# The order of the opening's loads, early pieces of the first gate products, and the bank of the third gate product in a fused attention and SwiGLU kernel

## The chip, the core and the metric

The kernel runs on one core of a Trainium2 chip. The metric is device time in microseconds. TensorE (PE) multiplies matrices into PSUM, ScalarE (ACT) evaluates functions, VectorE (DVE) does elementwise work, GpSimd (POOL) here only issues loads, and SyncE (SP) issues stores and transposing DMAs.

## What is computed

Sliding-window attention with a linear bias over 8 batches of 8 heads, 576 positions and 64 dimensions. Its output, 4608 tokens of 512 numbers, goes through a SwiGLU block.

```python
B, H, S, D = q.shape                                  # 8, 8, 576, 64
scores = np.matmul(q, k.transpose(0, 1, 3, 2)) / np.sqrt(D)
rel = pos[:, None] - pos[None, :]
mask = (rel >= 0) & (rel < 128)
scores = np.where(mask, scores - slopes[:, None, None] * np.abs(rel), -1e9)
attn = softmax(scores)
x = np.matmul(attn, v).transpose(0, 2, 1, 3).reshape(B * S, H * D)   # 4608 x 512
g, val = x @ w_gate, x @ w_val                        # 512 x 1536 each
out = (g * sigmoid(g) * val) @ w_out                  # 1536 x 512
```

## The kernel before

Attention works in tiles of 128 queries with all 8 heads. There are 36 tiles, nine for each pair of batches; the ninth holds the last 64 positions of both. A tile needs q, k and v of its rank, a block of 128 positions, and k and v of the rank before it. Its steps are these. q and k are transposed into `qT` and `kT` (L194 to L219: PE transposes into a bank `pt`, then a copy by VectorE, or by ScalarE for k from rank 4). The `scores` are multiplied into banks `ps` or `psc`, and ScalarE takes the exponential into `ex` (L288) or `exc` (L322). From tile 4 on VectorE multiplies by a mask (L294, L326). `weighted` (L330) multiplies with v into `av`, and VectorE divides into `x` (L353, L354). `x_transposed` (L364) puts x, transposed by PE through a bank `px`, into `xT`.

The feed-forward part works on blocks of 512 tokens, so block 0 is made of tiles 0 to 3 and block 1 of tiles 4 to 7. For each of 12 slices m of 128 columns, `wide` (L395) makes the gate product `pg` and the value product `pv`, four matmuls each. ScalarE takes a tanh of `pg` (`tt`, L421), VectorE makes `uu` (L422) and the product `hT` with `pv` (L433). `project` (L452) multiplies block 0's hT with the output weights into a bank `po`; later blocks use a form with seven products for eight.

A product can be made in pieces: `wide(n, m, which, c1)` makes the columns up to c1 that are still missing, and `early` remembers where it stopped. `begin(n, tiles)` (L822) does so for the first n of (m = 0 gate, m = 0 value, m = 1 gate, m = 1 value, ...). In `first_tiles` (L828) the opening's order is written by hand for PE, VectorE and ScalarE: after the scores of all four tiles, tile 3's `weighted`, then x of tile 2, `begin(4, 2)`, x of tile 3 and `begin(4, 3)`. The first eight steps of `ffn` (m = 0 to 3 of block 0) are in that hand order too. After them a scheduler interleaves the attention of later tiles with `ffn`, and `scored`, `target` and `ready` in the driver set how many attention steps go with each step of `ffn`. PE, VectorE and ScalarE each run their own queue in order, so whatever stands behind a waiting instruction waits as well.

All PSUM is in two pools. `ps_f` has the tag "gv" with three banks in rotation (pg, pv, and in the opening pt, av) and the tag "po" with one bank (in the opening pt of some q and px of tiles 0 to 3, later the projections). `ps_a` has the tag "a" with four banks (ps, psc, and from tile 4 on pt, av and px; also pg and pv of m = 0 and 1 of block 0, which `OTHER` names at L393). A bank is free again when its reader is done: for pg that is uu, for pv hT.

The loads of q, k, v and the weights are issued by POOL in the order of the program (L893 to L927), with eight in flight at a time: the trace gives them eight semaphores in turn, and a ninth is issued after the first has landed. They convert to 16 bits on the way. A load of q, k or v writes 128 KB, a piece of 256 gate or value columns 256 KB, four row blocks of the output weights 512 KB.

Of the kernel before, what the change touches and what calls it, by code (L numbers as in the profile page):

```python
# [10 lines left out]
FP32 = mybir.dt.float32  # L11
# [5 lines left out]
P = 128  # L17
# [10 lines left out]
FIRST = 4  # L28
# [10 lines left out]
def slot(h):  # L39

    return 4 * (h // 4) + 2 * (h % 2) + (h % 4) // 2
# [9 lines left out]
def kernel(  # L51
# [45 lines left out]
    def first_masks():  # L97
        nc.vector.tensor_copy(idf, idm)
        for h in by_slot:
            nc.scalar.mul(bias[:, slot(h), :], dist, -(2.0 ** (-8.0 * (h + 1) / H)) / scale)  # L100

    def later_masks():
        for h in by_slot:
            nc.scalar.activation(reg[:, slot(h), :], dist, AF.Exp, scale=-(2.0 ** (-8.0 * (h + 1) / H)))
# [36 lines left out]
    ps_f = ctx.enter_context(tc.tile_pool(name="ps_f", bufs=3, space=PSUM))  # L141
    ps_a = ctx.enter_context(tc.tile_pool(name="ps_a", bufs=4, space=PSUM))
# [26 lines left out]
    def source(src, rank):  # L169

        s, c = divmod(rank, 9)
        if c == 8:
            return [((64 * n, 64 * n + 64),
                     src[2 * s + n, :, 512:576, :].rearrange("h p d -> p h d")) for n in range(2)]
        b, t = 2 * s + c // 4, c % 4
        return [((0, P), src[b, :, t * P:(t + 1) * P, :].rearrange("h p d -> p h d"))]

    def load_v(rank):
        va[rank] = va_all[rank % NV]
        for (p0, p1), src in source(v, rank):  # L180
            nc.gpsimd.dma_start(va[rank][p0:p1, :, 0:D], src)  # L181

    def load_qk(rank, which="kq"):
        for name in which:
            t_ = nat.tile([P, H, D], FP16, name=name + "n", tag=name + "n")
            for (p0, p1), src in source(k if name == "k" else q, rank):
                nc.gpsimd.dma_start(t_[p0:p1], src)  # L187
            (natk if name == "k" else natq)[rank] = t_
# [141 lines left out]
    def weighted(i):  # L330

        s, p = units[i]
        x = xpool.tile([P, H, D], FP16, name="x", tag="x")
        xs[i] = x
        for half in range(2):
            pool, tag = (ps_f, "gv") if i < FIRST else (ps_a, "a")
            av = pool.tile([P, 4, D + 1], FP32, name="av", tag=tag)
            todo = []
            for j in range(4):
                h = 4 * half + j  # L340
                if p == 8:
                    for n, kt in enumerate((3, 7, 8)):
                        todo.append((j, ex[(s, "c", n)][:, slot(h), :], va[9 * s + kt][:, h, :]))
                else:
                    if p not in (0, 4):
                        todo.append((j, ex[(s, p - 1)][:, slot(h), 128:256],
                                     va[9 * s + p - 1][:, h, :]))
                    todo.append((j, ex[(s, p)][:, slot(h), 0:128], va[9 * s + p][:, h, :]))
            for n, (j, w, val) in enumerate(todo):
                nc.tensor.matmul(av[:, j, :], w, val, start=(n == 0), stop=(n == len(todo) - 1))  # L350
            rec = xpool.tile([P, 4, 1], FP32, name="rec", tag="rec", bufs=4)
            with tc.high_priority() if i in (6, 7) else ExitStack():
                nc.vector.reciprocal(rec, av[:, :, D:D + 1])  # L353
                nc.vector.tensor_mul(x[:, 4 * half:4 * half + 4, :], av[:, :, 0:D],  # L354
                                     rec.broadcast_to([P, 4, D]))
# [3 lines left out]
    def place(i):  # L359

        s, p = units[i]
        return (8, s) if p == 8 else (2 * s + p // 4, p % 4)

    def x_transposed(i):  # L364
        n, j = place(i)
        if n not in xT:
            xT[n] = bpool.tile([P, NKB, 512], FP16, name="xT", tag="xTc" if n == 8 else "xT",
                               bufs=1 if n == 8 else 3)
        x = xs.pop(i).rearrange("p h d -> p (h d)")
        dst = xT[n][:, :, j * P:(j + 1) * P]  # L370
        if i >= X_DMA_FROM:
            nc.sync.dma_start_transpose(dst, x)
            return
        pool, tag, n = (ps_f, "po", 1) if i < FIRST else (ps_a, "a", 4)
        pt = pool.tile([P, NKB, P], FP16, name="px", tag=tag, bufs=n)
        for kb in range(NKB):
            nc.tensor.transpose(pt[:, kb, :], x[:, kb * P:(kb + 1) * P], idm if i < FIRST else idm2)
        if i < FIRST:
            nc.vector.tensor_copy(dst, pt)
        else:  # L380
            nc.scalar.copy(dst, pt)
# [11 lines left out]
    OTHER = {(0, 0, "g"), (0, 0, "v"), (0, 1, "g"), (0, 1, "v")}  # L393

    def wide(n, m, which, c1=512):  # L395

        w, ms = wg_sb if which == "g" else wv_sb, slice(m * P, (m + 1) * P)
        ps, c0 = early.pop((n, m, which), (None, 0))
        if ps is None:
            pool, tag = (ps_a, "a") if (n, m, which) in OTHER else (ps_f, "gv")  # L400
            ps = pool.tile([P, 512], FP32, name="p" + which, tag=tag)
        for kb in range(NKB):
            nc.tensor.matmul(ps[:, c0:c1], w[:, kb, ms], xT[n][:, kb, c0:c1],  # L403
                             start=(kb == 0 and c0 == 0), stop=(kb == NKB - 1 and c1 == 512),
                             skip_group_check=(n <= 1))
        if c1 < 512:
            early[(n, m, which)] = (ps, c1)
        return ps
# [26 lines left out]
    def gate_val(n, m):  # L435
        c0 = 384 if (n, m) in acted else 0
        gate(n, m, wide(n, m, "g"), c0)
        yield
        val(n, m, wide(n, m, "v"), c0)
        yield  # L440
# [363 lines left out]
    def transposes_to(n):  # L804
        nonlocal done_t
        while done_t < n:
            transpose(done_t)
            done_t += 1
# [7 lines left out]
    def run(steps):  # L816
        for fs in steps:
            for f in fs:
                f()
            yield  # L820

    def begin(n, tiles, block=0):  # L822

        for m, which in ((0, "g"), (0, "v"), (1, "g"), (1, "v"), (2, "g"), (2, "v"))[:n]:
            if early.get((block, m, which), (None, 0))[1] < tiles * P:
                wide(block, m, which, tiles * P)

    def first_tiles():  # L828

        first_masks()  # L830
        transposes_to(need[0])
        for n, _ in enumerate(run(scores(0))):
            if n == 0:
                transposes_to(need[1])
        for i in range(FIRST):
            if i + 1 < FIRST:
                for n, _ in enumerate(run(scores(i + 1))):
                    if n == 0 and i + 2 < FIRST:
                        transposes_to(need[i + 2])
            else:  # L840
                later_masks()
            weighted(i)
            if 0 < i < FIRST - 1:
                x_transposed(i - 1)
        x_transposed(2)
        begin(4, 2)
        x_transposed(3)
        begin(4, 3)
# [35 lines left out]
    def load_w(c0, c1):  # L884
        for src, dst in ((wg2, wg_sb), (wv2, wv_sb)):
            nc.gpsimd.dma_start(dst[:, :, c0:c1], src[:, :, c0:c1])


    def load_wo(m0, m1):
        nc.gpsimd.dma_start(wo_sb[:, m0:m1, :], wo2[:, m0:m1, :])  # L890
# [14 lines left out]
    load_qk(4)  # L905
    load_qk(5, "q")
    load_w(512, 768)
    load_v(4)
    load_w(768, 1024)
    load_qk(5, "k")  # L910
    load_qk(6)
    load_v(5)
    load_w(1024, 1280)
    load_qk(7, "qk")
    load_v(6)
    load_w(1280, 1536)
    load_qk(8)
    load_wo(8, 12)
    load_v(7)
    load_wo(4, 8)  # L920
    load_qk(9)
    load_qk(10, "q")
    load_v(8)
    load_wo(0, 4)
    load_v(9)
    load_qk(10, "k")
    load_v(10)  # L927
# [27 lines left out]
    def everything():  # L955
# [3 lines left out]
        with tc.manual_schedule(engines=ENGINES[MANUAL]):  # L959
            first_tiles()  # L960
            done = FIRST
            steps = progress(ffn())
            while (at := next(steps)) < ALONE:
                if at == 2.0:
                    nc.scalar.copy(idm2, idm)
                if at in MASKS_AT:
                    make_mask(MASKS_AT.index(at))
# [54 lines left out]
```

The softmax here doesn't subtract the row's maximum and nothing guards it: scores larger than these inputs give would overflow.

## Time and profile before

| | |
|---|---|
| three runs | 337.87, 337.08, 337.05 us; median 337.08 |
| profiled run | 337.52 us, span of its instructions 335.7 us |
| granted TensorE clock | 1.00 |
| loads by POOL (software queue) | 118352 packets, 18.62 MB |

In the profile a line of the timeline gives start, duration (both us), engine, source line, operation, out<-in, the shape and the number of instructions merged; in brackets the idle time of the engine before it and what ended it. PEld is the weight load of PE, which overlaps its matmuls. Starts are from the beginning of the span.

The opening in time: the first load is issued at 1.24 us. Scores of tile 0 start at 7.87 and its exponentials at 8.29. The first gate matmul starts at 17.52, the first tanh at 20.81, and scores of tile 4 at 27.07. Block 0's last value product (m = 11) starts at 44.80. Scores of tile 9 start at 55.44, and the last load is issued before 200 us. From 240 us on only the feed-forward part is left.

The loads around the change, by the trace:

| load | issued | landed after |
|---|---|---|
| gate columns 0 to 256 | 10.09 | 5.4 |
| gate, value columns 512 to 768 | 15.64, 16.39 | 8.6, 9.2 |
| v of rank 4 | 17.27 | 9.3 |
| gate, value columns 768 to 1024 | 19.33, 20.62 | 9.1, 8.6 |
| k of rank 5, k of rank 6 | 21.60, 22.61 | 8.6, 8.5 |
| q of rank 6 | 23.47 | 8.4 |

### The profile page before, as it was taken

Reading aid. Unit: us, or ns where it says so; the run is one execution under the profiler, and the core shown is the slowest. Engines: PE = TensorE matmul, PEld = TensorE weight load, DVE = VectorE, ACT = ScalarE, POOL = GpSimd, SP = SyncE. Lnnn points to the kernel's source line nnn. Section 1 sums busy time; section 2 is a strip of 40 time slices with the busy share of each in tenths; the row PEclk is TensorE's granted clock in tenths of the full one; section 3 lists DMA queues with packets and bytes.
Section 4 is the critical chain, followed back from the end, with each engine's and each line's share of the span. In section 5 each row is a group of like instructions: output and inputs, shape, how many; then the busy total and the mean of one; then the engine's idle time right before and its main releaser. Section 6 shows DMA issues by size and latency. Waiting matters only on the chain.

```text
span 335.7 us, 7711 instructions
## 1 busy us (share of the span) xinstructions
PE 326.6 (97%) x2955; PEld 217.5 (65%) x2955; DVE 273.7 (82%) x643; ACT 208.0 (62%) x415; POOL 110.5 (33%) x137
## 2 busy tenths in 40 slices
PE   7999999999999999999999999999999999999994
PEld 3574455544456655656655655665788888888883
DVE  4668877999797779988999999999855985775683
ACT  4876768465665766666656466463577667676650
POOL 8977676357674282644226000000000000000000
PEclk9999999999999999999999999999999999999999
DMA  9999999999999999999999952030101101011014
GB/s 150 167 178 179 177 181 163 116 115 178 100 166 150 158 147 134 167 144 152 143 181 187 183 50 80 16 96 16 65 11 53 62 2 65 18 47 64 0 64 126
DMA packets 160053, 37.38 MB, mean 111 GB/s; under 512 B 147344, under 2 KB 155664, under 8 KB 160016
## 3 DMA queue, kind: packets, MB, share of 16 engines
q0 software_dynamic: 118352, 18.62, 89.8%
q1 hardware_dynamic: 40976, 17.64, 30.3%
q10 hardware_dynamic: 688, 0.62, 0.6%
q8 instruction: 23, 0.38, 0.5%
q14 instruction: 14, 0.11, 0.1%
HBM read 37.91 MB, written 9.44 MB: 141 GB/s over the span
## 4 chain that ended last, share of the span: by engine, by line
PE 69%; DVE 16%; DMA 5%; POOL 4%; issue 3%; ACT 2%; DVEq 0%; ACTq 0%; POOLq 0%
PE po L538 16%; PE pv L403 12%; PE pg L403 11%; PE gX L627 9%; PE gY L627 5%; PE av L350 3%; DVE uu L422 3%; DVE hT L433 3%; PE p L538 3%; PE ps L282 3%; DMA qn<-in_q_dram 2%; DMA wv_sb<-in_moe_w_val_dram 2%; PE gZ L627 2%; DVE ex L294 2%; PE po L457 2%
## 5 line engine op out<-in xcount | busy, mean ns | idle before, releaser
L403 PE MATMUL pv<-xT,wv_sb 128*128 128x512 f16 (+2 forms) x312 | 76.3, 363 | 0.5 <-DVE uu L422 0.4
L403 PE MATMUL pg<-xT,wg_sb 128*128 128x512 f16 (+3 forms) x316 | 76.0, 360 | 0.1
L421 ACT ACTIVATE tt<-pg 128x512 f16<-128x512 f32 x68 | 40.9, 603 | 45.4 <-PE pg L403 45.4
L288 ACT ACTIVATE ex<-ps 128x512 f16<-128x512 f32 x96 | 49.8, 607 | 7.1 <-PE ps L282 7.1
L422 DVE SCALAR_TENSOR_TENSOR uu<-tt,pg 128x512 f16<-128x512 f16 x67 | 45.6, 681 | 9.2 <-ACT tt L421 9.1
L433 DVE TENSOR_TENSOR hT<-uu,pv 128x512 f16<-128x512 f16 x68 | 46.2, 681 | 2.9 <-PE pv L403 1.3
L181 POOL DMA_DIRECT2D va<-in_v_dram x40 | 34.1, 857 | 30.6 <-DMA out_dram<-osb 11.1
L538 PEld LDWEIGHTS <-hT 128*128 128x128 f16 x384 | 37.2, 98 | 10.7 <-issue 0.8
L403 PEld LDWEIGHTS <-wv_sb 128*128 128x128 f16 x312 | 27.9, 98 | 24.8 <-issue 2.9
L403 PEld LDWEIGHTS <-wg_sb 128*128 128x128 f16 x316 | 28.2, 98 | 22.8 <-issue 1.7
L187 POOL DMA_DIRECT2D qn<-in_q_dram x39 | 33.3, 859 | 19.9 <-DMA va<-in_v_dram 12.9
L187 POOL DMA_DIRECT2D kn<-in_k_dram x39 | 33.3, 857 | 17.3 <-DMA qT<-qn 6.6
L538 PEld LDWEIGHTS <-S 128*128 128x128 f16 x288 | 27.4, 98 | 7.3 <-issue 1.4
L294 DVE TENSOR_TENSOR ex<-ex,m_reg 128x1024 f16<-128x1024 f16 x42 | 28.5, 685 | 2.3 <-ACT ex L288 2.3
L354 DVE TENSOR_TENSOR x<-av,rec 128x256 f16<-128x256 f32 x72 | 28.5, 419 | 0.4
L538 PE MATMUL po<-T,S 128*128 128x256 f16 x192 | 25.9, 273 | 0.3 <-ACT u2s L564 0.3
L538 PE MATMUL po<-T,hT 128*128 128x256 f16 x192 | 26.0, 272 | 0.1
L322 ACT ACTIVATE exc<-psc 128x512 f16<-128x512 f32 x40 | 21.3, 606 | 2.7 <-PE psc L318 2.7
L681 DVE TENSOR_TENSOR hT<-s,v 128x512 f16<-128x512 f16 x18 | 7.6, 424 | 17.7 <-ACT s L680 17.7
L350 PEld LDWEIGHTS <-ex 128*128 128x128 f16 x384 | 17.4, 97 | 3.9 <-issue 0.4
L350 PE MATMUL av<-va,ex 128*128 128x65 f16 x384 | 19.3, 193 | 0.0
L282 PE MATMUL ps<-qT,kT 64*128 64x256 f16 x192 | 16.4, 272 | 0.1
(129 smaller groups left out, 533.5 us busy)
## 6 DMA issues: line engine op xcount, KB each, us to landing
out_dram<-osb SPq DMA_DIRECT2D x32, 256.0 KB, 2.4
va<-in_v_dram POOLq DMA_DIRECT2D x32, 128.0 KB, 8.2
qn<-in_q_dram POOLq DMA_DIRECT2D x31, 128.0 KB, 8.6
kn<-in_k_dram POOLq DMA_DIRECT2D x31, 128.0 KB, 8.5
wg_sb<-in_moe_w_gate_dram POOLq DMA_DIRECT2D x6, 256.0 KB, 7.8
wv_sb<-in_moe_w_val_dram POOLq DMA_DIRECT2D x6, 256.0 KB, 8.2
wo_sb<-in_moe_w_out_dram POOLq DMA_DIRECT2D x3, 512.0 KB, 8.7
kn<-in_k_dram POOLq DMA_DIRECT2D x8, 64.0 KB, 7.5
```

The source lines that it names most:

```text
L181: nc.gpsimd.dma_start(va[rank][p0:p1, :, 0:D], src)
L187: nc.gpsimd.dma_start(t_[p0:p1], src)
L288: nc.scalar.activation(e[:, o:o + 2, :], banks[q4][par], AF.Exp, scale=scale)
L294: nc.vector.tensor_mul(e[:, o, :], e[:, o, :], reg[:, o, :])
L350: nc.tensor.matmul(av[:, j, :], w, val, start=(n == 0), stop=(n == len(todo) - 1))
L354: nc.vector.tensor_mul(x[:, 4 * half:4 * half + 4, :], av[:, :, 0:D], rec.broadcast_to([P, 4, D]))
L403: nc.tensor.matmul(ps[:, c0:c1], w[:, kb, ms], xT[n][:, kb, c0:c1], start=(kb == 0 and c0 == 0), stop=(kb == NKB - 1 and c1 == 512), skip_ ...
L421: nc.scalar.activation(tt, pg[:, c0:c1], AF.Tanh, scale=0.5)
L422: nc.vector.scalar_tensor_tensor(out=uu, in0=tt, scalar=one if (n, m) == PIN else 1.0, in1=pg[:, c0:c1], op0=ALU.add, op1=ALU.mult)
L433: nc.vector.tensor_mul(hT[n][:, m, c0:c1], acted[(n, m)][1][:, c0:c1], pv[:, c0:c1])
L538: nc.tensor.matmul(dst, a[:, m, cols], b[:, m, :], start=(start and m == 0), stop=(m == HM - 1), skip_group_check=True)
L627: nc.tensor.matmul(dst[:, i, :], w[:, kb, c0 + i * P:c0 + (i + 1) * P], a[:, kb, :], start=(start and i == 0 and kb == 0), stop=(i == 1 an ...
```

## The change

It has three parts.

First, the order of POOL's loads between the second block of gate and value columns and rank 10. v of ranks 4, 5 and 8 and k of ranks 6 and 7 go later. The gate and value columns 768 to 1536, q of ranks 6 and 7, and the last output-weight rows (0 to 4) go earlier. No load is added or dropped.

Second, ahead of tile 3's `weighted`, the first 128 columns of the gate products of m = 0 and m = 1 are made; `begin(4, 2)` then makes only the second 128 of these two. Their banks are those of "a".

Third, banks. px of tile 2 takes one of the three "gv" banks instead of "po", and the gate product of block 0, m = 3 takes "po" instead of "gv". The fourth argument of the pool call is now given for all; its values are those that held before.

```diff
-        pool, tag, n = (ps_f, "po", 1) if i < FIRST else (ps_a, "a", 4)
+        pool, tag, n = ((ps_f, "gv", 3) if i == 2 else (ps_f, "po", 1) if i < FIRST
+                        else (ps_a, "a", 4))
...
-            pool, tag = (ps_a, "a") if (n, m, which) in OTHER else (ps_f, "gv")
-            ps = pool.tile([P, 512], FP32, name="p" + which, tag=tag)
+            pool, tag, bufs = ((ps_a, "a", 4) if (n, m, which) in OTHER
+                               else (ps_f, "po", 1) if (n, m, which) == (0, 3, "g")
+                               else (ps_f, "gv", 3))
+            ps = pool.tile([P, 512], FP32, name="p" + which, tag=tag, bufs=bufs)
...
             else:
                 later_masks()
+                for m in range(2):
+                    wide(0, m, "g", P)
             weighted(i)
...
     load_qk(5, "q")
     load_w(512, 768)
-    load_v(4)
     load_w(768, 1024)
     load_qk(5, "k")
-    load_qk(6)
+    load_qk(6, "q")
+    load_w(1024, 1280)
+    load_v(4)
+    load_qk(6, "k")
+    load_qk(7, "q")
     load_v(5)
-    load_w(1024, 1280)
-    load_qk(7, "qk")
+    load_w(1280, 1536)
+    load_qk(7, "k")
     load_v(6)
-    load_w(1280, 1536)
     load_qk(8)
...
     load_qk(10, "q")
+    load_wo(0, 4)
     load_v(8)
-    load_wo(0, 4)
     load_v(9)
```

The scheduler that orders the later steps sees the changed banks and loads, so the order of PE's instructions changes as well, between the third gate product and about the third piece of block 1's first products. There several products of block 0 come ahead of the transposes and scores of tiles 4 to 6 where they stood behind them.

## The prediction

> **What bounds the kernel now.** I read the page's shares first, then the busy table by stretch, then TensorE's waits up to 64 us, then the opening's timeline.
>
> ```profile
> PE 326.6 (97%) x2955; PEld 217.5 (65%) x2955; DVE 273.7 (82%) x643; ACT 208.0 (62%) x415; POOL 110.5 (33%) x137
> ...
> DVE  4668877999797779988999999999855985775683
> ...
> DMA  9999999999999999999999952030101101011014
> ```
>
> TensorE is the bound, and the DMA engines are full until about 195 us: more loads at once are not to be had, only another order of them.
>
> ```profile
> 28.00:32.00 4.00, 3.34 (x20) 1.57 (x19) 3.45 (x6) 2.99 (x7) 2.79 (x4) 1.00 2.18 166
> 32.00:36.00 4.00, 4.00 (x27) 1.83 (x27) 2.91 (x5) 2.68 (x6) 3.12 (x5) 1.00 1.99 174
> ...
> 60.00:80.00 20.00, 19.92 (x153) 10.03 (x152) 19.88 (x45) 11.54 (x21) 10.02 (x12) 1.00 1.99 125
> ```
>
> Columns: window, its length, then PE, PEld, DVE, ACT and POOL busy with counts. From 60 us TensorE hardly rests, so what can be won lies before; from 60 to 80 VectorE is as full as TensorE.
>
> ```profile
> PE pt L214 <- DMA qn<-in_q_dram: 0.9, 2, 0.7
> ...
> PE pv L403 <- DVE uu L422: 0.4, 2, 0.3
> PE av L350 <- ACT exc L322: 0.2, 1, 0.2
> ...
> PE px L377 <- DVE xT L379: 0.2, 1, 0.2
> ```
>
> The same four on the timeline (start, duration, idle before):
>
> ```profile
> 16.51 0.20 PE L350 MATMUL av<-va,exc 128*128 128x65 f16 x1 [0.22 <-ACT exc L322]
> 17.30 0.38 PE L377 MATMUL px<-idm,x 128*128 128x128 f16 x4 [0.22 <-DVE xT L379]
> 24.96 1.02 PE L403 MATMUL pv<-xT,wv_sb 128*128 128x512 f16 x4 [0.26 <-DVE uu L422]
> 31.90 0.40 PE L214 MATMUL pt<-idm,qn 128*128 128x128 f16 x4 [0.66 <-DMA qn<-in_q_dram]
> ```
>
> A matmul's end is modelled some 0.16 us late, so I count start to start, less the undisturbed spacing of that shape (0.216 us for 512 columns, 0.109 for 256, 0.055 for 128, 0.029 for 65: medians of this trace). The four losses are then 0.39, 0.38, 0.43 and 0.82, and 0.25 more at 36.74.
>
> **What the Trainium skill says.** "TensorE: Matmul & The Clock Gate", section Back-to-back issue gap, gives N/2.4 + 2.5 ns, 216 for 512 columns and 56 for 128; the trace has 216 and 55. "DMA: Bandwidth & Descriptors", Issuing engines are not separate DMA queues: all queues share the same 16 DMA engines. The full DMA row agrees. "PSUM — Partial Sum Buffer", Specifications (TRN2), counts eight banks in a partition; the pools hold 3 ("gv") + 1 ("po") + 4 ("a"), all of them, so a bank can only be borrowed. "Perfetto Trace Analysis", Optimization Strategy, advises finding the gaps of the bounding engine and the semaphore behind each; that is done below.
>
> **The change, part by part.** The listing of both programs' instruction orders agrees on PE, DVE and ACT up to the second x transpose, differs up to the third piece of (block 1, m = 0), about 55 us, and is the same to the end. So I follow TensorE to that point. PE's work is equal up to eight more weight loads and matmuls: eight gate matmuls of 256 columns become sixteen of 128.
>
> *Fill, and the px bank.* Eight 128-column matmuls (8 x 0.055 = 0.44) go ahead of the products of tile 3, at 16.03; their weights landed at 15.50 (issue 10.09, 5.4 to landing) and the first xT copy was done at 15.76 (15.35 + 0.41). They fill the 0.39 before 16.51: the products end near 16.95 instead of 16.92, and the saved columns (8 x 0.054 = 0.43) are taken off later. px of tile 2 now takes a "gv" bank, free with x itself (16.49 + 0.43 = 16.92), so it runs at 16.98; the gate matmuls after it still need the second xT copy (16.83 + 0.41, seen at 17.30). They start at 17.30 instead of 17.52: 0.22. With the 0.43 this is 0.65, and small pieces make it 0.68: (0, 2, gate), at 21.28 before, starts at 20.60. The first tanh moves from 20.81 to 20.13, VectorE's first uu from 21.44 to 20.76.
>
> *The idle bank, m = 3.* (0, 3, gate) takes "po", idle until the first projection at 51.5, so (0, 3, value) finds px's "gv" bank free (copied by 18.67) and the 0.43 at 24.96 and 0.07 at 25.89 go. (0, 4, gate) is now next, at 24.05, ahead of the transposes of k4, q4, q5. It waits for uu of m = 2: from 20.76 five VectorE operations (0.79 + 0.61 + 0.79 + 0.61 + 0.68, the spacing at 21.44 to 24.23), done at 24.23; and for gate columns 512 on, which land at 24.23. So it starts at 24.28, losing 0.23. Net 0.27, total 0.95. What queues behind this new wait are those transposes and scores of tile 4: 27.06 before, about 27.85 now.
>
> *Loads.* Between the value columns 512 to 768 (landing 25.56) and q of rank 6 (31.86) stand now three loads instead of five: v4 and k6 go behind. These two took 1.01 and 0.96 between landings, so q6 lands near 29.9; TensorE, 0.95 ahead and with other work first, wants it at 30.15. Of 0.82 at 31.90 at most 0.1 is left. But qT of rank 6 now comes after uu of m = 6, at 31.85 to 32.27, and scores of tile 5 start at 32.32 where TensorE was ready at 32.06: 0.24 lost. Total 0.95 + 0.82 - 0.1 - 0.24 = 1.43. What is moved back has room: v4 lands near 33.4 (needed 34.8), k6 34.2 (38.0), v5 36.0 (40.5), gate columns 1280 on 37.2 (38.8), wo rows 0 to 4 near 53.6 (about 54.2).
>
> *What is given back.* From 33 to 43 us VectorE sets the pace: 0.16 before (0, 8, value) and 0.25 before (0, 9, value), against the 0.25 of before. At scores of tile 6 (39.74 against 39.97) ScalarE now has a tanh (m = 10) ahead of the four exponentials, which end it at 40.40, just where they start before; the products of tile 5 need a bank that the first exponential frees, 41.05 in both. Total 1.09 at 43.7. Tiles 7 and 8 keep that; the last x copy of block 1 now stands behind kT's on ScalarE (before: 54.04 for x, 54.52 for kT), so the gate piece that needs it starts at 53.75, not 54.68: **0.93 us** at the point where the orders meet.
>
> *After it.* VectorE was idle before 55.73 (0.60), so it owes nothing there, and from then on all wait for each other in the same order. k of rank 10 landed at 57.2 and is transposed at 66.8, so loads leave room. The same loads go through POOL, the tiles' later ones at the same places, and SP's queue keeps its order; POOL's first wait after 57 us (6.6 us, for SP's transposes) shows it ahead of need. I carry 0.93 to the end at full size.
>
> The span here is 335.7; the runs are 337.05 to 337.87, the profiled run 337.52, so about 1.4 lie outside the span. 337.08 - 0.93 = 336.15.
>
> **Bounds of what the trace does not show.** The fill: from +0.44 (all on the path) to -0.39; I take the whole wait, as its inputs are 0.3 early. The m = 3 bank: 0 to -0.50, I take -0.27. Loads: +0.2 to -0.82, I take -0.48 with qT's wait. Middle: +0.6 to -0.25, I take +0.5.
>
> **Rivals.** *All waits go.* 0.68 + 0.50 + 0.82 + 0.25 = 2.25: 334.8. For it: the four waits are real and VectorE is idle over 20% up to 56 us. Against it: VectorE runs in bursts, and scores move behind FFN pieces. *Attention's chain decides.* If exponentials, masks and x of tiles 6 and 7 arrive as before, TensorE, in order, stands at block 1 until the last x copy, and 0.3 at most is left: 336.9. For it: exponentials at 40.40 in both; against it: scores of tiles 7 and 8 come 1.4 earlier in my account. *The late value tile.* v4 goes behind k5, q6 and two weight loads. TensorE needs it at 34.8, everything behind it waits, one for one. Slower than 338.1 takes a landing after 34.8 + 0.93 + 1.0 = 36.7, 3.3 later than I expect: 338.5. The full DMA row speaks for it, the other three landings that the order leaves early against it. *That the fill isn't made* is excluded by the order.
>
> **How the numbers follow.** My account 0.52 (335.6 to 336.7), all waits go 0.22, attention's chain 0.19, the late tile 0.07. What a measurement can tell from no change is 0.3%, 1.01 us: the border 336.07 cuts my account just above its middle, so faster is 0.22 + 0.28 = 0.50, same 0.24 + 0.19 = 0.43, slower 0.07. The range, 334.9 to 337.2, leaves the late tile and a tail at each end outside.
>
> **What will show it.** No wait at the products of tile 3; the first tanh near 20.1; (0, 4, gate) near 24.3 after uu; q6 without a wait over 0.2; the four exponentials of tile 6 at 40.4; the third gate piece of block 1 near 53.75, with the same distance kept at the end. I am wrong if that piece comes before 53.2 or after 54.3, or if the lead changes after it.

## The result and the profile after

The changed kernel takes 336.04 us (median; 335.91 to 336.21), the kernel before, run beside it, 337.13 (337.05 to 337.87). The ratio is 0.9963 with a 95% interval of 0.9946 to 0.998: 1.09 us less, where 0.93 was forecast. The profiled span went from 335.7 to 334.1 us; that is more than the medians differ by, as the profiled execution of before was itself a long one (337.52 us).

First the busy shares of the page, the VectorE row and the DMA row in 40 slices:

```profile
PE 326.4 (98%) x2963; PEld 218.1 (65%) x2963; DVE 274.1 (82%) x643; ACT 207.8 (62%) x415; POOL 110.3 (33%) x137
...
DVE  4678878999797879987999999999855985775683
...
DMA  9999999999999999999979912030101101011014
```

The work is what it was, up to eight matmuls (2963 for 2955). The DMA row is about as full as before (one slice near 170 us reads 7): the loads are the same, only their order changed.

The busy table by stretch (window, length, then PE, PEld, DVE, ACT and POOL busy with counts):

```profile
28.00:32.00 4.00, 4.00 (x30) 1.94 (x27) 3.56 (x7) 3.32 (x7) 2.86 (x5) 1.00 1.78 182
32.00:36.00 4.00, 3.77 (x30) 2.00 (x30) 2.91 (x6) 3.04 (x6) 3.13 (x5) 1.00 2.11 170
60.00:80.00 20.00, 19.89 (x155) 9.91 (x153) 19.85 (x44) 11.04 (x20) 10.22 (x12) 1.00 1.83 136
```

From 28 to 32 us TensorE is now busy all 4.00 us (3.34 before). A hole of 0.23 has opened in the next window. From 60 to 80 us TensorE and VectorE are as busy as before, to within 0.03 us.

TensorE's waits up to 64 us:

```profile
PE av L350 <- ACT ex L288: 0.3, 1, 0.3
...
PE ps L282 <- DVE qT L219: 0.2, 1, 0.2
PE pt L214 <- DMA qn<-in_q_dram: 0.2, 1, 0.2
PE pv L406 <- DVE uu L425: 0.2, 1, 0.2
```

The 0.2 for `qn` is the load at 6.66 us, which the change doesn't touch; the 0.7 of q of rank 6 is gone. So are the waits for `exc` and `xT` in the opening, and of the two for `uu` one is left. New are one for `qT` and one for `ex`. Where they are, the timeline tells (start, duration, idle before):

```profile
16.02 0.61 PE L406 MATMUL pg<-xT,wg_sb 128*128 128x128 f16 x8
...
16.96 0.40 PE L378 MATMUL px<-idm,x 128*128 128x128 f16 x4
17.28 0.38 PE L406 MATMUL pg<-xT,wg_sb 128*128 128x128 f16 x4
...
20.14 0.60 ACT L424 ACTIVATE tt<-pg 128x512 f16<-128x512 f32 x1 [1.26 <-PE pg L406]
...
24.30 1.02 PE L406 MATMUL pg<-xT,wg_sb 128*128 128x512 f16 x4
...
30.15 0.39 PE L214 MATMUL pt<-idm,qn 128*128 128x128 f16 x4
...
32.28 0.61 PE L282 MATMUL ps<-qT,kT 64*128 64x256 f16 x8 [0.23 <-DVE qT L219]
...
39.77 0.60 ACT L424 ACTIVATE tt<-pg 128x512 f16<-128x512 f32 x1 [0.34 <-PE pg L406]
40.27 2.06 ACT L288 ACTIVATE ex<-ps 128x512 f16<-128x512 f32 x4
40.91 0.40 PE L350 MATMUL av<-va,ex 128*128 128x65 f16 x8 [0.31 <-ACT ex L288]
...
53.48 0.38 PE L406 MATMUL pg<-xT,wg_sb 128*128 128x128 f16 x4
...
54.24 0.61 PE L282 MATMUL ps<-qT,kT 64*128 64x256 f16 x8
```

The fill stands at 16.02 and the products of tile 3 follow it without a wait. The transposes of q of rank 6 run at 30.15 with nothing before them. Scores of tile 5 (32.28) wait for `qT`. At 39.77 a tanh goes ahead of the exponentials of tile 6, and the products at 40.91 wait for the first of these. Scores of tile 9 start at 54.24, 55.44 before.

### The profile page after: what moved, and what is told of

It is laid out like the page before. It is cut to its first block, busy times and chain, and to the rows that moved or that the text cites. A ratio compares the mean times of both kernels' runs of the same rounds, so it can differ in the third digit from the quotient of the medians.

```text
span 334.1 us, 7729 instructions
## 1 busy us (share of the span) xinstructions
PE 326.4 (98%) x2963; PEld 218.1 (65%) x2963; DVE 274.1 (82%) x643; ACT 207.8 (62%) x415; POOL 110.3 (33%) x137
## 4 chain that ended last, share of the span: by engine, by line
PE 87%; DVE 7%; ACT 2%; DMA 2%; issue 1%; DVEq 0%; POOLq 0%
PE po L541 19%; PE pg L406 17%; PE pv L406 16%; PE gX L630 9%; PE av L350 5%; PE gY L630 5%; PE ps L282 3%; PE p L541 3%; PE gZ L630 2%; DVE uu L425 2%; PE px L378 2%; PE psc L318 2%; DVE hT L436 2%; DMA qn<-in_q_dram 2%; PE po L460 2%
## 5 line engine op out<-in xcount | busy, mean ns | idle before, releaser
L406 PE MATMUL pg<-xT,wg_sb 128*128 128x512 f16 (+2 forms) x324 | 76.5, 355 | 0.1
L187 POOL DMA_DIRECT2D kn<-in_k_dram x39 | 33.4, 860 | 21.8 <-DMA qT<-qn 6.5
```

## Experiments

The change has four separable edits: the load order (L), the eight early gate matmuls (F), the "gv" bank for px of tile 2 (PX), and the idle bank for the gate product of m = 3 (M3). Eight kernels take some of them away, three more change loads alone. Two numbers are given for each. The first is the gain in runs: the median of before in the same comparison (337.23 for e1 to e4, 337.21 for e5 to e8, 337.12 for e9 to e11 and 337.13 us for the changed kernel) less the kernel's own. The second is the lead in the trace at the scores of tile 9, where the instruction orders have met again. In before these start at 55.44 and the scores of tile 0 at 7.87, so 47.57 apart; the lead is 47.57 less the same distance in the kernel. The scores of tile 0 are taken off because their start differs by up to 0.35 us between single executions (below). For the changed kernel it is 47.57 - (54.24 - 7.85) = 1.18. The two lines of before are

```profile
7.87 0.61 PE L282 MATMUL ps<-qT,kT 64*128 64x256 f16 x8
...
55.44 0.61 PE L282 MATMUL ps<-qT,kT 64*128 64x256 f16 x8
```

In between, where the orders differ, the lead is read by TensorE columns done: the time at which before has started its n-th column less the time at which the kernel has, with each matmul counted by its undisturbed spacing and nothing taken off for the start.

| kernel | edits | median us | ratio, 95% interval | gain in runs | lead in trace |
|---|---|---|---|---|---|
| e1_loads | L | 336.65 | 0.9982, 0.9975 to 0.9989 | 0.58 | 0.62 |
| e2_no_loads | F, PX, M3 | 337.34 | 1.0003, 0.9995 to 1.0011 | -0.11 | -0.05 |
| e3_fill | F | 337.21 | 0.9997, 0.9989 to 1.0005 | 0.02 | 0.17 |
| e4_banks | PX, M3 | 337.50 | 1.0006, 0.9998 to 1.0015 | -0.27 | -0.15 |
| e5_no_fill | L, PX, M3 | 336.68 | 0.9985, 0.9977 to 0.9993 | 0.53 | 0.76 |
| e6_no_banks | L, F | 336.23 | 0.9968, 0.9956 to 0.998 | 0.98 | 1.05 |
| e7_no_m3 | L, F, PX | 335.98 | 0.9961, 0.9949 to 0.9974 | 1.23 | 1.27 |
| e8_no_px | L, F, M3 | 336.47 | 0.9975, 0.9966 to 0.9985 | 0.74 | 0.95 |
| changed kernel | all | 336.04 | 0.9963, 0.9946 to 0.998 | 1.09 | 1.18 |

### The loads alone, and all but the loads

e1_loads is the kernel before with the new order of loads and nothing else:

```diff
     load_w(512, 768)
-    load_v(4)
     load_w(768, 1024)
     load_qk(5, "k")
-    load_qk(6)
-    load_v(5)
+    load_qk(6, "q")
     load_w(1024, 1280)
-    load_qk(7, "qk")
-    load_v(6)
+    load_v(4)
+    load_qk(6, "k")
+    load_qk(7, "q")
+    load_v(5)
     load_w(1280, 1536)
+    load_qk(7, "k")
+    load_v(6)
...
-    load_v(8)
     load_wo(0, 4)
+    load_v(8)
```

> The new order of loads alone; the orders of TensorE, VectorE and ScalarE stay those of before. My account: q of rank 6 lands near 29.8 and the 0.82 wait at 31.90 goes, so scores of tile 5 start near 32.1 instead of 32.88; of this some 0.2 to 0.3 is given back before block 1. 0.5 faster than before (0.2 to 0.8), about 336.6. If attention's chain of exponentials decides: under 0.2 faster. If every wait removed counts in full: 0.8 faster.

e2_no_loads is the changed kernel with the old order of loads:

> The changed kernel with the loads in the order of before: fill and both banks stay. My account: the landing of q of rank 6 is a fixed date, 31.86. TensorE is 0.95 ahead before it and waits there about 1.7 until 31.9, so scores of tile 5 start near 33.7 with four more products of 512 columns done, which is no lead at all: 337.1 (336.7 to 337.4). If fill and banks count by themselves, whatever the loads: 0.9 faster, 336.2.

Measured: 0.58 us won by the loads alone, and nothing (-0.11, the interval spans 1) by everything else without them. The scores of tile 5 and what stands ahead of them, in before:

```profile
32.14 0.81 PE L403 MATMUL pv<-xT,wv_sb 128*128 128x512 f16 x3
32.88 0.61 PE L282 MATMUL ps<-qT,kT 64*128 64x256 f16 x8
```

The timeline of e1_loads there:

```profile
31.14 0.39 PE L214 MATMUL pt<-idm,qn 128*128 128x128 f16 x4
...
32.33 0.61 PE L282 MATMUL ps<-qT,kT 64*128 64x256 f16 x8 [0.16 <-DVE qT L219]
```

and that of e2_no_loads at the same transposes of q of rank 6:

```profile
31.71 0.40 PE L214 MATMUL pt<-idm,qn 128*128 128x128 f16 x4 [1.34 <-DMA qn<-in_q_dram]
```

In e1_loads the wait of 0.82 for q is gone and one for `qT` has come in its place, 0.32 start to start where before had 0.09 in the same spot (32.88 - 32.14 less three spacings of 0.216): 0.82 - 0.23 = 0.59. In e2_no_loads TensorE arrives 0.87 ahead at q of rank 6, finds it not landed, and stands until 31.71; it started at 31.90 before. In the four kernels with the old order q landed at 31.86 (before), 31.66 (e2), 31.78 (e3) and 31.72 (e4), although TensorE came to it at 31.08, 30.21, 30.73 and 30.58; with the new order it landed between 29.61 and 30.15. So here the landing is set by the load's place in the order, not by when TensorE comes, and every gain made ahead of it is waited away there: of its 0.87 e2_no_loads keeps about 0.2, by which q happened to land earlier.

### The fill alone, and the banks alone

e3_fill is before with the two lines of the fill, e4_banks is before with both bank edits:

```diff
             else:
                 later_masks()
+                for m in range(2):
+                    wide(0, m, "g", P)
             weighted(i)
```

> The eight early 128-column matmuls alone, loads and banks as before. My account: the third gate product starts at 20.85 instead of 21.28 (the 0.39 wait is filled, the px wait stays), VectorE's first uu 0.43 earlier, and all of it is eaten at q of rank 6, 31.86: 337.1 (336.8 to 337.3). If it counts by itself: 0.43 faster, 336.7.

```diff
-        pool, tag, n = (ps_f, "po", 1) if i < FIRST else (ps_a, "a", 4)
+        pool, tag, n = ((ps_f, "gv", 3) if i == 2 else (ps_f, "po", 1) if i < FIRST
+                        else (ps_a, "a", 4))
...
+                               else (ps_f, "po", 1) if (n, m, which) == (0, 3, "g")
```

> Both banks alone (px of tile 2 in gv, third gate product in po), loads as before and no early matmuls. My account: px at 16.96 and gates after it at 17.3 instead of 17.52, then the wait of 0.43 at 24.96 goes; about 0.5 ahead at q of rank 6, where all of it is eaten: 337.1 (336.8 to 337.4). If it counts by itself: 0.5 faster, 336.6.

Measured: 0.02 and -0.27. The wait at q of rank 6, start to start, is 1.09 in e3_fill and 1.18 in e4_banks, 0.82 before: the same sink. What is left behind the wait (at 36 us, by columns done, 0.10 and 0.14) stays to 55 us in e3_fill and turns to -0.13 in e4_banks; why, the next part shows. The 337.50 of e4_banks lies just above its forecast range. One reading lesson lies in e3_fill, whose timeline is

```profile
31.82 0.40 PE L214 MATMUL pt<-idm,qn 128*128 128x128 f16 x4 [0.92 <-ACT kT L217]
```

The releaser named is ScalarE's copy of kT. That copy reads another bank (that of the transposes just before, in a rotation of four), began at 31.21 and was done at 31.79; q landed at 31.78. Two events 0.01 apart can't be told apart here (e4_banks has the same, with 31.75 and 31.72). Before settles it: there the same copy ran from 31.55 to 32.13, and the transposes of q started at 31.90, ahead of its end. The traces of before and of e2_no_loads name the load, and e1_loads, which moves only loads, is rid of the wait.

### One edit taken from the whole

e5_no_fill leaves out the fill, e6_no_banks both bank edits, e7_no_m3 the idle bank for m = 3, e8_no_px the "gv" bank for px of tile 2. Each diff is the matching part of the change, reversed; that of e7_no_m3:

```diff
-            pool, tag, bufs = ((ps_a, "a", 4) if (n, m, which) in OTHER
-                               else (ps_f, "po", 1) if (n, m, which) == (0, 3, "g")
-                               else (ps_f, "gv", 3))
-            ps = pool.tile([P, 512], FP32, name="p" + which, tag=tag, bufs=bufs)
+            pool, tag = (ps_a, "a") if (n, m, which) in OTHER else (ps_f, "gv")
+            ps = pool.tile([P, 512], FP32, name="p" + which, tag=tag)
```

> The changed kernel without the eight early matmuls (new loads and both banks stay). My account: TensorE starts the third gate product 0.22 to 0.25 earlier than before instead of 0.68; the lead where the orders meet falls from 1.20 to about 0.77: 0.75 faster than before (0.5 to 1.0), 336.5. If the fill is worth nothing, because VectorE sets the pace from 33 us on: as the changed kernel, 1.2 faster.

> New loads and the eight early matmuls, px of tile 2 and the third gate product in the banks of before; the order from 21 us on is that of before. My account: 0.57 from the loads alone plus 0.43 from the fill, which is not eaten at q of rank 6 now (lands 29.8, wanted near 30.7): 1.0 faster (0.8 to 1.1), 336.2. If the bank for m = 3 is what carries the lead past 25 us: 0.6 to 0.7 faster.

> The changed kernel with the third gate product back in gv; new loads, fill and the px bank stay, and the order from 21 us on is that of before. My account: 0.57 from the loads plus the 0.68 of the opening, 1.25 faster (1.0 to 1.35), 336.0, no worse than the changed kernel: what the idle bank gains at 24.96 its reordering gives back between 33 and 45 us. If the idle bank is worth the 0.27 that I gave it: 0.9 faster.

> The changed kernel with px of tile 2 back in po; new loads, fill and the bank for m = 3 stay. My account: px waits until 17.30 again, the third gate product starts at 20.85 instead of 20.6, and the lead falls from 1.20 to 0.95: 0.95 faster than before (0.75 to 1.1), 336.3. If VectorE's pace decides: as the changed kernel.

With the new loads in place F and PX count. Added one after the other, L gives 0.58; F on top of it 0.98 - 0.58 = 0.40; PX on top of both 1.23 - 0.98 = 0.25. M3 takes 0.14 off again (1.23 to 1.09), and 0.24 off where PX is missing (0.98 to 0.74). Each of these two is within the intervals, but in neither pair does M3 win. e5_no_fill (0.53) against the whole (1.09) says 0.56 for the fill, more than its hole; its lead in the trace (0.76 against 1.18) says 0.42. Likewise e8_no_px (0.74, just below its forecast range) says 0.35 for PX, not 0.25. The sizes hold to 0.1 or 0.2, which is within the intervals.

Where M3's gain goes can be read in the traces. In e7_no_m3 the wait of the value product of m = 3 for a bank stays (0.43 start to start), as before the change:

```profile
24.29 1.02 PE L404 MATMUL pv<-xT,wv_sb 128*128 128x512 f16 x4 [0.26 <-DVE uu L423]
...
39.11 2.06 ACT L288 ACTIVATE ex<-ps 128x512 f16<-128x512 f32 x4
...
39.76 0.40 PE L350 MATMUL av<-va,ex 128*128 128x65 f16 x8
...
41.34 0.60 ACT L422 ACTIVATE tt<-pg 128x512 f16<-128x512 f32 x1 [0.16 <-PE pg L404]
```

The changed kernel has no such wait, but 0.23 at 24.30, and then 0.27 at 37.15 and 0.48 at 40.91, where e7_no_m3 has 0.23 at 35.46 and 0.24 within the scores of tile 6. Only the kernels with M3 have a different order of instructions on TensorE, VectorE and ScalarE; F adds its eight matmuls, and L and PX leave the order as it is, so of the loads and banks that the scheduler sees it is the bank of m = 3 alone that moves it. In M3's order the tanh of m = 10 (39.77) is ahead of the exponentials of tile 6; in e7_no_m3 it is behind them (41.34). The exponentials start at 40.27 where e7_no_m3 has them at 39.11, and the products of tile 5 at 40.91 instead of 39.76. Other pieces were moved ahead of them, so this is no loss of 1.15; but of the 0.26 that the changed kernel leads e7_no_m3 by at 30 us (0.93 against 0.67, by TensorE columns done), -0.09 is left at 55 us. The size is the same wherever M3 is: from 36 to 55 us the lead falls by 0.24 to 0.28 in all five kernels with it (the changed kernel, e2, e4, e5, e8), with a lead of 1.46 or of 0.14 to start from, and by nothing beyond 0.03 in e1, e3, e6 and e7. So M3's order takes back about the 0.26 that its bank wins, and where the gain has been waited away at q of rank 6, as in e2 and e4, it is a loss. That the tanh is what does it was not isolated: no kernel was run with M3's banks and the other order.

### Which of the moved loads counts

e9_only_q6 is e7_no_m3 in which, of the loads up to rank 8, only q of rank 6 is brought forward; behind it these loads follow as before (the output-weight rows 0 to 4 stay where the change has them):

```diff
     load_w(768, 1024)
     load_qk(5, "k")
     load_qk(6, "q")
-    load_w(1024, 1280)
     load_v(4)
     load_qk(6, "k")
-    load_qk(7, "q")
     load_v(5)
-    load_w(1280, 1536)
-    load_qk(7, "k")
+    load_w(1024, 1280)
+    load_qk(7, "qk")
     load_v(6)
+    load_w(1280, 1536)
```

> As the kernel without the idle bank (early matmuls, px bank, new loads; 0.9961 of before), but of the loads between columns 512 and rank 8 only the part that brings q of rank 6 forward is kept: v of rank 4 and k of rank 6 stand behind it, and v5, columns 1024 on, q and k of rank 7, v6 and columns 1280 on follow in the order of before. My account: one date mattered here, q6's. q6 lands near 29.9; gate columns 1024 near 33.9 (needed 34.1), value columns 1024 near 35.1 (needed 35.5), gate columns 1280 near 39.2 (needed 40.0): no new wait over 0.1, so 0.996 to 0.9965 of before, -1.1 to -1.3 us. Rival, every one of the moved loads earns its share: a weight piece comes late at 34.1 or 40.0, and the gain falls to -0.8 or less.

Measured: 336.04 us, ratio 0.997 (0.996 to 0.9981), a gain of 1.08; lead in the trace 1.30. e7_no_m3 has 1.23 and 1.27: no difference that the intervals could tell. q landed at 30.04, the weight columns from 1024 on at 33.68 and 35.04, and TensorE's waits are those of e7_no_m3. Of the loads up to rank 8 one date mattered, q's. That the weights go ahead of v4, k6 and q7 neither gains nor costs anything that these intervals could show. The gain of 1.08 is just short of the 1.1 to 1.3 expected.

### How much room the late loads have

e10_late_v4 is e7_no_m3 with v of rank 4 three loads later, behind k6, q7 and v5 (the expectation says two); e11_late_wo is e7_no_m3 with the output-weight rows 0 to 4 behind v of rank 8, as before the change.

```diff
     load_w(1024, 1280)
-    load_v(4)
     load_qk(6, "k")
     load_qk(7, "q")
     load_v(5)
+    load_v(4)
```

> As the kernel without the idle bank (0.9961 of before), with v of rank 4 two loads later, behind v of rank 5. It then lands near 36.2 where TensorE wants it at 34.97. If a late value tile costs one for one, TensorE stands 1.2 there, of which the wait of 0.2 at 35.5 is saved: 1.0 lost, 0.999 of before (-0.2 us). If VectorE and ScalarE set the pace from 33 to 43 us (attention's chain decides), they run on during the wait and most of it is made up by 55 us: -0.8 or better.

```diff
-    load_wo(0, 4)
     load_v(8)
+    load_wo(0, 4)
     load_v(9)
```

> As the kernel without the idle bank (0.9961 of before), with the output-weight rows 0 to 4 behind v of rank 8, as before the change. They then land near 55.3 where TensorE wants them at 54.7: 0.6 lost at 55 us, carried to the end, 0.998 of before (-0.6 to -0.7 us). Rival, the wait falls together with the 0.33 that TensorE waits right behind it at 55.2 and the loads' lateness is hidden: -0.9 to -1.2 us.

Measured: 337.03 us for e10_late_v4, ratio 0.9998 (0.999 to 1.0007), gain 0.09, lead 0.29; and 336.27 us for e11_late_wo, ratio 0.9976 (0.9965 to 0.9986), gain 0.85. The timeline of e10_late_v4:

```profile
36.34 0.43 PE L350 MATMUL av<-va,ex 128*128 128x65 f16 x8 [1.14 <-DMA va<-in_v_dram]
...
38.54 0.60 ACT L422 ACTIVATE tt<-pg 128x512 f16<-128x512 f32 x1 [2.70 <-PE pg L404]
```

and of e11_late_wo:

```profile
54.28 0.61 PE L282 MATMUL ps<-qT,kT 64*128 64x256 f16 x8
55.77 0.38 PE L458 MATMUL po<-wo_sb,hT 128*128 128x512 f16 x1 [0.88 <-DMA wo_sb<-in_moe_w_out_dram]
55.99 1.02 PE L404 MATMUL pv<-xT,wv_sb 128*128 128x512 f16 x4
```

v of rank 4 landed at 36.30 and TensorE started 0.04 later, having stood 1.30. Of that, 0.23 came back from the wait behind it, which was gone, and 0.1 by 39 us from smaller pauses; the lead fell from 1.27 to 0.29, and the runs lost 1.05 to 1.14. Nothing more was made up in the 16 us from there to the meeting point. VectorE and ScalarE could not use the time: ScalarE was idle for 2.70 us before the tanh at 38.54, for want of a gate product (1.62 before the same tanh in e7_no_m3), and VectorE stood 0.41 for the late products. So the late value tile cost its full lateness less 0.3, and in this order VectorE doesn't set the pace from 33 to 55 us.

The output weights landed at 55.73. TensorE stood 1.10 there, and 0.33 that it waits right behind in e7_no_m3 went: the lead is 1.28 at the scores of tile 9 and 0.66 at the value product after them ((56.53 - 7.87) - (55.99 - 7.99)). That is 0.62 in the trace, as expected, but only 0.29 to 0.38 in the runs, between the expectation and the rival. The traced execution was one of the longest of its kernel (336.67 us, median 336.27), and this landing is no fixed date: with the rows at the same place it came at 55.32 in before, 55.09 in e2, 54.27 in e3 and 54.33 in e4. A landing before 54.7 would have cost nothing. That it comes earlier in most runs of e11_late_wo is likely, but not shown. Moving these rows forward is thus worth about 0.3 in the runs, and only together with the other edits: before the change they landed at 55.32 and were wanted at 55.98, and with a lead of 1.27 they are wanted at 54.7.

## Why the prediction was right

The steps, as forecast and as found in the changed kernel:

| step | forecast | found |
|---|---|---|
| products of tile 3 | no wait, behind the fill at 16.03 | no wait, fill at 16.02 |
| px of tile 2; second gate pieces | 16.98; 17.30 | 16.96; 17.28 |
| first tanh; (0, 2, gate) | 20.13; 20.60 | 20.14; 20.61 |
| (0, 4, gate), after uu of m = 2 | 24.28 | 24.30 |
| q of rank 6 landed; wanted | 29.9; 30.15 | 29.79; 30.15 |
| scores of tile 5, after qT | 32.32, 0.24 lost | 32.28, 0.40 start to start, 0.09 of it as before |
| v of rank 4 landed | 33.4 | 33.53 |
| exponentials of tile 6 | 40.40 | 40.27 |
| third gate piece of block 1 | 53.75 | 53.48 |

**The opening and q's landing.** The account ran 0.68, then 0.95, then 1.43. By TensorE columns done the lead is 0.67 at 22 us, 0.93 at 30 and 1.46 at 36. These are right to 0.03, and the runs agree with the sizes one by one, as far as they resolve them: 0.40 (or 0.56) for F against 0.43 to 0.46, 0.25 (or 0.35) for PX against 0.22.

**The loads** were mis-sized by a little. Taken were 0.82, less up to 0.1 left of the wait, less 0.24 for qT (32.32 less 32.06 is 0.26): 0.48. Nothing of the wait was left, and the new order alone won 0.58.

**What is given back** is the term that was off: 0.50 from 33 us on (1.43 to 0.93). Measured is 1.46 at 36 us to 1.20 at tile 9 (55.44 - 54.24), so 0.26. The steps that it named were there. Before the value products at 35.16 and 37.15 TensorE lost 0.12 and 0.27 (forecast 0.16 and 0.25), the tanh of m = 10 did stand ahead of the exponentials of tile 6, and the last x copy behind that of kT. Two of the sizes were too large: the products of tile 5 started at 40.91, not 41.05, and the third gate piece lost 0.06 more than before at the last x copy, not 0.16. What the account did not see is whose loss it is. It booked the m = 3 bank as a gain of 0.27 and the middle as a term of its own, and the expectation for e1_loads takes such a term off without M3 too. But the kernels without M3 (e1_loads, e6_no_banks, e7_no_m3) give nothing back: by columns done the lead of e7_no_m3 is 1.27 at 33 us, 1.29 at 43 and 1.30 at 55. The loss belongs to M3's order. So the m = 3 bank and the middle are one step: forecast 0.27 - 0.50 = -0.23, found -0.09 in the trace and -0.14 in the runs (1.09 less 1.23). With 0.68 for F and PX and 0.6 for the loads this gives 1.19 in the trace, where 1.18 is read. So 0.93 was low by two terms, by 0.12 (loads) and 0.14 (bank and middle) in the trace. That the runs, at 1.09, come closer to it than the trace is no merit of the account.

**The end.** The lead kept its size: the last matmul starts at 329.72 against 330.94, which is 1.22 as it stands, 1.20 at tile 9. The two signs of being wrong stayed away: the third gate piece came at 53.48, within 53.2 to 54.3, and the lead did not change after it.

**The rivals.** *All waits go* (2.25) fell: the changed kernel still waits 0.23, 0.40, 0.27 and 0.48 at 24.30, 32.28, 37.15 and 40.91. *Attention's chain decides* (0.3 at most) fell: in the changed kernel the exponentials of tile 6 come at 40.27, only 0.13 earlier than before, and the lead is 1.18 all the same; in e7_no_m3 the exponentials of tile 6 start at 39.11, 1.29 earlier than the 40.40 of before, and the lead is 1.27. *The late value tile* fell for this order, with the landing at 33.53 and the use at 34.8; e10_late_v4 shows its price where it does come late: 1.0 for a wait of 1.30.

## What to carry to other kernels

When TensorE waits for a load later on, as at q of rank 6 here, every gain ahead of that wait is only waited away there: move the load first, then count the others, and test edits of an opening together with the loads they run into. Move a load forward only as far as the one pushed back still lands before its use, since a late one stops TensorE: v of rank 4 cost 1.0 for a wait of 1.30, the output-weight rows 0.6 for one of 1.10 in the trace, the difference being later waits that fell away. A freed bank can lead a scheduler to another order, and is then worth what that order is worth, not the wait that it removes; read it where the orders meet again, not where the wait was.

## What was not expected of the hardware

The scores of tile 0 start anywhere from 7.85 to 8.20 us in the traces of these kernels, though all instructions up to there are the same, and what an execution loses there it can carry along, if TensorE waits for no load behind it: e9_only_q6, the latest at 8.20, has its fill at 16.35 (16.02 in the changed kernel), and its last matmul at 329.90, 0.30 behind e7_no_m3, whose runs it equals within the intervals. Where 0.3 us matter, single traces are to be compared from a common start. Landings differ too: the output-weight rows 0 to 4, at the same place of the old order, landed anywhere from 54.27 to 55.73 us in five traces, q of rank 6 only from 31.66 to 31.86 in four.

Even so, in all but one of the kernels the trace shows more lead than the runs, by 0.04 to 0.23 us (e11_late_wo shows 0.19 less behind its wait). Before was traced once, in an execution of 337.52 us where its medians are 337.08 to 337.23, and in that trace q of rank 6 landed 0.08 to 0.20 us later than in e2, e3 and e4, which have the same load order. TensorE waits for it there, so before's trace is some 0.1 slow at that point, which accounts for about that much of the surplus in every lead. The rest stays open.
